# VectorE's share of the exponentials: a chain of ten short steps in place of six, with a new pacing

## The chip, the cores and the metric

The kernel runs on one core of one Trainium2 chip. The metric is the device time of one execution in microseconds (us); with several runs the median is given. TensorE is called PE (PEld is its weight load), VectorE DVE, ScalarE ACT, GpSimd POOL and SyncE SP, as the profile names them.

## The reference

Four transformer attention layers on one sequence of 2048 rows of 640 features, in bf16: layers 0 and 2 look at a sliding window of 256 keys, layers 1 and 3 at all keys. There are 32 heads of 20 features.

```python
def block(x, wqkv, wo, windowed):
    q, k, v = split_heads(x @ wqkv)                 # 32 heads, 20 features each
    scores = einsum("bhqd,bhkd->bhqk", q, k) * 20 ** -0.5
    if windowed:
        scores = where((i - j >= 0) & (i - j < 256), scores, -1e9)
    return merge_heads(softmax(scores) @ v) @ wo

x = x + block(layernorm(x), A_wqkv, A_wo, True)     # layer 0
x = x + block(layernorm(x), B_wqkv, B_wo, False)    # layer 1
x = x + block(layernorm(x), A_wqkv, A_wo, True)     # layer 2
x = x + block(layernorm(x), B_wqkv, B_wo, False)    # layer 3
```

The softmax is computed without subtracting a maximum. Its exponentials are the bulk of the elementwise work: one for each head, query and key.

## The kernel before

**Units and banks.** The sequence is cut into 4 chunks `c` of 512 queries and the heads into 8 groups `g` of 4. A *unit* is the attention of one layer, chunk and group. Its work is a list of *banks*: one bank is the scores of 128 keys by 512 queries for one head, which fills one PSUM bank. A unit of layers 1 and 3 has 16 key blocks by 4 heads, 64 banks; a windowed unit (layers 0 and 2) has 12. Chunk 0 of layers 1 and 3 is computed in parts, whose partial sums are kept in the tile `raw_o`.

**The tiles of the main loop.** The loop (L1269 on) takes three banks at a time, a *tile* (a turn of the loop, called a tick in the code). For each tile, PE computes the scores (L1308) into one of two sets of PSUM banks (0 to 2, or 3 to 6), ACT takes the exponential of the whole tile (L1339) into a tile `pt`, and two or three turns later PE multiplies `pt` with the values (L1373) into PSUM bank 7, which adds up over the unit and is copied out by DVE at its end (L857). In odd turns of the late part a tile can have four banks, if bank 6 is free and no other work wants it. Windowed tiles are multiplied with masks by DVE (L1410).

**The work between.** Layer norm, projections, output projection (L552) and the unit ends run as generators which the loop advances a little in each turn. From about 480 us on, when layer 1 has left its first chunk, all of them share PSUM bank 6: PE writes it, DVE takes the result out (L314, L561, L1048, L1064, L1085), and the next of them may use it. Every engine works through its own instructions in the order in which this program emits them, so a PE instruction that waits for DVE to empty a bank holds back all PE instructions behind it. PE also gets multiplications whose result nobody reads (L634), which keep its clock up.

**Exponentials on DVE.** For most units of layers 1 and 3 with c > 0, the banks of the last key block are taken out of ACT's list: heads 2 and 3 in layer 1 (`aside = (2, 3)`, 24 units, one pair each), all four heads in layer 3 (22 units, two pairs each). They make 68 pairs. The generator `t_side` computes them on DVE, a pair of banks (1024 elements on each of 128 partitions) at a time. The score, scaled by log2(e), becomes an integer whose bits are those of a float: the exponent field gives a power of two, the fraction field goes through a polynomial, and the two are multiplied. The steps of a pair:

- L910, twice: PSUM to integer. In layer 1 the scores were computed as the third bank of a normal tile, which stands in a fixed plan. In layer 3 the generator itself issues the matmul (L903) into bank 6, in odd turns only, and then books bank 6 for two turns.
- L915 and L920: fraction bits and exponent bits.
- L925, L929 and L933: the polynomial, each step `(a op scalar) op b` over two 4-byte tiles.
- L941: the last polynomial step times the power of two, written in bf16 as the pair's output.

PE reads the pair's output at the end of the unit (L1382).

**Pacing.** Each step of `t_side` yields a cost in credit, 0.7 or 1.2. Once in a turn, behind the products with the values, the credit grows by `SIDE_RATE` (late, layer 3) or by 0.4 (before), up to 1.2, and steps are emitted while it is above zero. At a step "bank" the generator stops until a turn in which the scores can be had. `side_done` and `side_need` push the generator on at a unit's end if its pairs are not ready.

**Buffers.** In the middle stage the scratch tiles `xi`, `xm`, `xw` lie in `raw_o` (groups 0 to 5), and groups 6 and 7 are two output pairs. In layer 3 the scratch lies in three of the five `xnT` tiles, which layer norm no longer needs, and three output pairs lie in `ka`.

Of the kernel before, what the change touches and what calls it, by code (L numbers as in the profile page):

```python
# [9 lines left out]
BF16 = mybir.dt.bfloat16  # L10
F32 = mybir.dt.float32
I32 = mybir.dt.int32
ALU = mybir.AluOpType
ACT = mybir.ActivationFunctionType

P = 128
# [5 lines left out]
KD = D // P  # L22
G = 8
C = 512
NC = S // C
EPS = 1e-5
SCALE = DH ** -0.5
# [4 lines left out]

E23 = 2.0 ** 23
LOG2E = 1.4426950408889634
EA, EB, EC, ED = -0.10468731, 1.17604568, 0.83196789, 0.24582313
KA = 18
SIDE_RATE = 0.85
QA = 4

PARTS = {  # L40
# [6 lines left out]
def kernel(  # L47
# [14 lines left out]
    def pool(name, bufs, space=None):  # L62
        kw = {"space": space} if space else {}
        return ctx.enter_context(tc.tile_pool(name=name, bufs=bufs, **kw))
# [5 lines left out]
    xtp = pool("xtp", 5)  # L70
# [34 lines left out]
    op = ps[:, 7, :]  # L105
# [10 lines left out]
    for h in range(2):  # L116
        for n in range(2):
            a = n * D + h * HD
# [10 lines left out]
    def load_wop(w, dense):  # L129
# [9 lines left out]
        out=ident[:], in_=ident[:], compare_op=ALU.not_equal, fill=1.0,  # L139
# [6 lines left out]
    for m, b, ge in (  # L146
# [4 lines left out]
        v = masks[:, m, b * P : (b + 1) * P]  # L151
        nc.gpsimd.affine_select(
            out=v, in_=v, compare_op=ALU.is_ge if ge else ALU.is_gt, fill=0.0,
# [139 lines left out]
    live = Counter()  # L293
# [81 lines left out]
    xnT = {}  # L375
# [491 lines left out]
    side = {"credit": 0.0, "gen": None, "tiles": None, "late": False}  # L867

    def side_start():

        assert live["xnT"] == 0
        tl = [xtp.tile([P, KD, C], BF16, name="xnT", tag="xnT") for _ in range(3)]
        live["xnT"] += 3
        f = [v[:, 0:4, :].rearrange("p a b -> p (a b)") for v in tl[0:3]]
        side["tiles"] = [v.bitcast(F32) for v in f]
        side["out"] = deque(ka_all[:, KA - 6 + 2 * n : KA - 4 + 2 * n, :] for n in range(3))
        side["late"] = True

    def side_early():

        b = part_o["t"]
        side["tiles"] = [b[:, 2 * n : 2 * n + 2, :].rearrange("p a b -> p (a b)") for n in range(3)]
        side["out"] = deque(
            b[:, n, :].bitcast(BF16).rearrange("p (a b) -> p a b", a=2) for n in (6, 7)
        )
        side["gen"] = t_side()
        side_step(False)

    def t_side():

        V = nc.vector
        while aside:
            u = aside[0]
            for pair in range(len(u.aside) // 2):
                while id(u) not in loaded or (u.l == 3 and not side["late"]):
                    yield None
                for i in range(2):
                    yield "bank"
                    xi, xm, xw = side["tiles"]
                    if u.l == 3:  # L900
                        mseq[0] += 1
                        mfree[6] = (state["tick"] + 2, mseq[0])
                        nc.tensor.matmul(  # L903
                            ps[:, 6, :], lhsT=u.k(NT - 1, u.aside[2 * pair + i]),
                            rhs=u.q(u.aside[2 * pair + i], 0, 4), start=True, stop=True,
                        )
                        side["psum"] = ps[:, 6, :]
                    scored = side.setdefault("scored", {})
                    scored[id(u)] = scored.get(id(u), 0) + 1
                    V.tensor_scalar(  # L910
                        out=xi.bitcast(I32)[:, i * C : (i + 1) * C], in0=side["psum"],
                        scalar1=SCALE * LOG2E * E23, scalar2=-128.0 * E23, op0=ALU.mult, op1=ALU.max,
                    )
                    yield 0.7
                V.tensor_scalar(  # L915
                    out=xm.bitcast(I32), in0=xi.bitcast(I32), scalar1=0x7FFFFF, scalar2=0x3E800000,
                    op0=ALU.bitwise_and, op1=ALU.bitwise_or,
                )
                yield 0.7
                V.tensor_scalar(  # L920
                    out=xi.bitcast(I32), in0=xi.bitcast(I32), scalar1=0x7F800000,
                    scalar2=0x40000000, op0=ALU.bitwise_and, op1=ALU.bitwise_xor,
                )
                yield 0.7
                V.scalar_tensor_tensor(  # L925
                    out=xw, in0=xm, scalar=EA, in1=xm, op0=ALU.add, op1=ALU.mult
                )
                yield 1.2
                V.scalar_tensor_tensor(  # L929
                    out=xm, in0=xw, scalar=EB, in1=xm, op0=ALU.mult, op1=ALU.add  # L930
                )
                yield 1.2
                V.scalar_tensor_tensor(  # L933
                    out=xw, in0=xw, scalar=EC, in1=xm, op0=ALU.add, op1=ALU.mult
                )
                yield 1.2
                while not side["out"]:
                    yield None
                pt = side["out"].popleft()
                po = pt.rearrange("p a b -> p (a b)")  # L940
                V.scalar_tensor_tensor(  # L941
                    out=po, in0=xw, scalar=ED, in1=xi, op0=ALU.add, op1=ALU.mult
                )
                side_out.setdefault(id(u), []).append(pt)
                yield 1.2
            aside.popleft()

    def side_step(bank):

        if side["gen"] is None:  # L950
            return False
        moved = False
        while True:
            if side.get("at") == "bank" and not bank:
                return moved
            if side["credit"] <= 0.0:
                return moved
            try:
                at = side["at"] = next(side["gen"])
            except StopIteration:  # L960
                side["gen"] = None
                return moved
            if at is None:
                return moved
            moved = True
            if at == "bank":
                if not bank:
                    return moved
                continue
            side["credit"] -= at  # L970
            if bank:
                return moved
# [223 lines left out]
    with tc.manual_schedule():  # L1196
# [12 lines left out]
        tiles = []  # L1209
        starts = {}  # L1210
        n = 0
# [57 lines left out]
        while ended is None or t < ended + 8:  # L1269
# [3 lines left out]
            if t < len(tiles) or banks:  # L1273
                if t >= len(tiles) and not side["late"] and not live["xnT"] and not todo:
                    side_start()
# [36 lines left out]
                if cur[-1][2] == "side":  # L1312
                    cur = cur[:-1]
                    n_b -= 1
                    if side["gen"] is None:
                        side_early()
                    while side["at"] != "bank":
                        side["credit"] = 0.1
                        assert side_step(False)
                    side["credit"] = max(side["credit"], 0.1)  # L1320
                    side["psum"] = sp[:, n_b, :]
                    side_step(True)
# [11 lines left out]
                while i < n_b:  # L1334
                    b0 = cur[i][3]
                    k = i
                    while k < n_b and cur[k][3] == b0:
                        k += 1
                    nc.scalar.activation(  # L1339
                        out=pt[:, i:k, b0 * P :], in_=sp[:, i:k, b0 * P :],  # L1340
# [50 lines left out]
                    break  # L1391

            if n_b:
                side["credit"] = min(side["credit"] + (SIDE_RATE if side["late"] else 0.4), 1.2)
                side_step(False)

            if t > 0 and masked is not None:
                cur_, pt_ = masked
                i = 0
                while i < len(cur_):  # L1400
# [4 lines left out]
                    if m is not None:  # L1405
# [5 lines left out]
                            out=pt_[:, i:k, cols], in0=pt_[:, i:k, cols], in1=mv_, op=ALU.mult  # L1411
# [38 lines left out]
```

## Time and profile before

| | |
|---|---|
| runs | 2284.01, 2285.57, 2287.35 us |
| median | 2285.57 us |
| the profiled execution | 2284.01 us |
| its span, first to last instruction | 2282.3 us |
| mean granted PE clock | 0.864 |
| exponentials on ACT (L1339) | 1638 instructions, 2096.5 us |
| of these four banks wide | 27 |
| side steps on DVE (L910 to L941) | 544 instructions, 520 us |

The side rows by shape, summed: L910 93.8 us in 136 instructions, L915 and L920 94.4 in 136, L925 to L941 331.5 in 272.

How to read the page: it shows one execution, with the busy time of each engine; then the span cut into 40 equal slices with the busy share of each in tenths, where PEclk is the clock that PE was granted; then groups of equal instructions as "line engine operation written<-read shape xcount | busy us, mean ns of one | idle us of the engine just before them <-who ended it". A list of waits has "engine, what it was about to do <- what it waited for: us in all, times, longest". A table by stage has, for each stretch of time, the busy us and instruction count of PE, PEld, DVE, ACT and POOL, and then the granted clock, the DMA share and GB/s.

### The profile page before, as it was taken

What the parts mean: (1) busy time and instruction counts of PE and PEld (TensorE: products, weight loads), DVE (VectorE), ACT (ScalarE), POOL (GpSimd) and SP (SyncE); (2) the same over time, 40 slices, a digit from 0 to 9 for tenths busy, and PEclk for the clock granted to TensorE, in tenths of its full rate; (3) what the DMA queues carried; (4) which work ended last, traced back from release to release, by engine and by line L of the source; (5) the groups of instructions that cost most, each with busy time, mean ns of one, the idle gap of its engine ahead of it and who ended that gap; (6) DMA issues with size and microseconds to landing.
All of it is one profiled execution on the core that took longest, in us unless ns stands there. A gap on an engine that the chain in (4) does not pass through costs nothing.

```text
span 2282.3 us, 40030 instructions
## 1 busy us (share of the span) xinstructions
PE 1978.4 (87%) x15586; PEld 704.1 (31%) x15746; DVE 1272.2 (56%) x2214; ACT 2169.6 (95%) x1741; POOL 271.0 (12%) x445
## 2 busy tenths in 40 slices
PE   8899999989898998888888998898878888888887
PEld 3343343333233333233332333232221122122222
DVE  6667675435454566455564643432555565666662
ACT  7789899999999999999899999999999999999997
POOL 4323223201100122001210022011000000000000
PEclk9899999999999999999999999999755565556556
DMA  6223223322210233002320043012111111111100
GB/s 193 78 69 101 81 83 90 97 75 56 70 33 14 61 96 93 15 27 64 101 71 14 16 116 95 28 44 74 54 47 30 30 42 30 30 39 41 35 17 15
DMA packets 88284, 135.16 MB, mean 59 GB/s; under 512 B 20766, under 2 KB 63486, under 8 KB 88094
## 3 DMA queue, kind: packets, MB, share of 16 engines
q1 hardware_dynamic: 68878, 79.43, 12.6%
q0 software_dynamic: 19216, 53.17, 7.8%
q8 instruction: 123, 2.02, 0.4%
q14 instruction: 67, 0.55, 0.1%
HBM read 99.52 MB, written 27.79 MB: 56 GB/s over the span
## 4 chain that ended last, share of the span: by engine, by line
ACT 45%; PE 30%; issue 16%; DVE 9%; DMA 0%; ACTq 0%; POOL 0%; SPq 0%; DVEq 0%; POOLq 0%
ACT pt L1339 44%; PE ps L1308 7%; PE ps L364 6%; PE ps L552 5%; PE ps L1373 4%; PE ps L465 3%; DVE pt L1410 2%; PE ps L634 1%; DVE st L314 1%; DVE on L1085 1%; ACT ka L1339 1%; PE ps L1081 1%; DVE x_sb L561 1%; PE ps L429 0%; DVE raw_o L910 0%
## 5 line engine op out<-in xcount | busy, mean ns | idle before, releaser
L1339 ACT ACTIVATE pt<-ps 128x1536 bf16<-128x1536 f32 (+2 forms) x1638 | 2096.5, 1478 | 74.2 <-PE ps L1308 64.9
L1308 PE MATMUL ps<-qt,kt 32*128 32x512 bf16 x4008 | 635.9, 451 | 176.7 <-ACT pt L1339 144.6
L1373 PE MATMUL ps<-pt,vt 128*21 128x512 bf16 x3852 | 462.5, 452 | 7.1 <-issue 4.5
L1308 PEld LDWEIGHTS <-kt 32*128 32x128 bf16 x4008 | 186.0, 93 | 594.1 <-issue 575.7
L1410 DVE TENSOR_TENSOR pt<-pt,masks 128x1024 bf16<-128x1024 bf16 (+6 forms) x403 | 209.5, 554 | 151.0 <-ACT pt L1339 150.5
L634 PE MATMUL ps<-masks,ident 128*128 128x512 bf16 x708 | 243.5, 387 | 27.7 <-DVE on L1085 7.1
L364 PE MATMUL ps<-xnT,wqk 128*128 128x512 bf16 x761 | 206.3, 382 | 19.2 <-DVE on L1085 3.9
L1373 PEld LDWEIGHTS <-vt 128*21 128x21 bf16 x3960 | 99.5, 90 | 337.4 <-issue 325.1
L314 DVE CAST st<-ps 128x512 bf16<-128x512 f32 x134 | 92.7, 692 | 183.8 <-PE ps L364 169.9
L552 PE MATMUL ps<-wop,on 128*128 128x320 bf16 x928 | 165.0, 317 | 8.3 <-DVE x_sb L561 5.2
L910 DVE TENSOR_SCALAR xnT<-ps 128x512 int32<-128x512 f32 x88 | 60.9, 692 | 185.8 <-PE ps L903 185.8
L1308 PE MATMUL ps<-qa,ka 32*128 32x384 bf16 (+2 forms) x1408 | 118.2, 278 | 27.7 <-ACT pt L1339 22.0
L1085 DVE TENSOR_TENSOR on<-on,ps 128x512 bf16<-128x512 bf16 x128 | 86.4, 685 | 65.8 <-PE ps L1081 64.7
L561 DVE TENSOR_TENSOR x_sb<-x_sb,ps 128x320 bf16<-128x320 bf16 x120 | 58.1, 484 | 115.1 <-PE ps L552 114.9
L857 DVE CAST on<-ps 128x512 bf16<-128x512 f32 x112 | 77.1, 688 | 75.1 <-PE ps L1373 48.3
L465 PE MATMUL ps<-wv,xnT 128*128 128x320 bf16 x640 | 110.6, 301 | 7.9 <-DVE on L1085 3.1
L552 PEld LDWEIGHTS <-on 128*128 128x128 bf16 x928 | 84.0, 101 | 77.0 <-issue 47.8
L364 PEld LDWEIGHTS <-wqk 128*128 128x128 bf16 x830 | 69.9, 97 | 111.3 <-issue 53.9
L634 PEld LDWEIGHTS <-ident 128*128 128x128 bf16 x798 | 59.7, 96 | 132.6 <-issue 131.2
L398 POOL TENSOR_SCALAR rstd<-mv 128x4 f32<-128x4 f32 x15 | 4.1, 277 | 776.6 <-DVE mv L385 755.9
L1373 PE MATMUL ps<-pt,va 128*21 128x384 bf16 (+2 forms) x1408 | 75.6, 282 | 3.9 <-DVE pt L1410 1.6
L1308 PEld LDWEIGHTS <-ka 32*128 32x128 bf16 x1408 | 43.0, 92 | 95.9 <-issue 85.9
(101 smaller groups left out, 1585.1 us busy)
## 6 DMA issues: line engine op xcount, KB each, us to landing
vt<-v_d SPq DMA_DIRECT2D x48, 336.0 KB
kt<-k_d SPq DMA_DIRECT2D x192, 80.0 KB
wqk<-in_B_wqkv_dram POOLq DMA_DIRECT2D x80, 160.0 KB, 3.5
wqk<-in_A_wqkv_dram POOLq DMA_DIRECT2D x70, 160.0 KB, 3.4
k_d<-st POOLq DMA_DIRECT2D x75, 128.0 KB, 2.1
q_d<-st POOLq DMA_DIRECT2D x75, 128.0 KB, 2.1
qt<-q_d SPq DMA_DIRECT2D x384, 20.0 KB
v_d<-vs POOLq DMA_DIRECT2D x16, 336.0 KB, 3.0
```

The costliest lines, as they stand in the source:

```text
L314: nc.vector.tensor_copy(out=out_, in_=in_)
L364: nc.tensor.matmul(pq, lhsT=wt[:, dc, :], rhs=xt[:, dc, :], start=(dc == 0), stop=(dc == KD - 1),)
L465: nc.tensor.matmul(pv, lhsT=xt[:, dc, i * P : (i + 1) * P], rhs=wv_sb[l % 2][:, dc, h * HD : (h + 1) * HD], start=(dc == 0), stop=(dc == K ...
L552: nc.tensor.matmul(yp, lhsT=on[:, g, qb * P : (qb + 1) * P], rhs=wop[:, g, i * HD : (i + 1) * HD], start=(g == a), stop=(g == b - 1),)
L561: nc.vector.tensor_tensor(out=xv, in0=had, in1=yp, op=ALU.add)
L634: nc.tensor.matmul(ps[:, b, :], lhsT=ident[:], rhs=masks[:, 0, :], start=True, stop=True)
L857: nc.vector.tensor_copy(out=oT, in_=op)
L1085: nc.vector.tensor_tensor(out=oT, in0=oT, in1=zb, op=ALU.mult)
L1308: nc.tensor.matmul(sp[:, i, col * P : (col + qn) * P], lhsT=u.k(kc, j), rhs=u.q(j, q0, qn), start=True, stop=True,)
L1339: nc.scalar.activation(out=pt[:, i:k, b0 * P :], in_=sp[:, i:k, b0 * P :], func=ACT.Exp, scale=SCALE,)
L1373: nc.tensor.matmul(op[32 * j : 32 * j + VW, q0 * P : (q0 + qn) * P], lhsT=u.v(kc, j), rhs=pg[:, i, col * P : (col + qn) * P], start=(first ...
L1410: nc.vector.tensor_tensor(out=pt_[:, i:k, cols], in0=pt_[:, i:k, cols], in1=mv_, op=ALU.mult)
```

## The change

The chain of a pair is written anew. The integer now carries the float's bias (L910 adds 127 x 2^23 instead of clamping). The fraction is mapped to 1..2 instead of 0.25..0.5. The power of two is cut out by one bit operation and then clamped at zero by a separate step into a new bf16 tile `xe`. The polynomial of fourth degree is evaluated as (y^2 + EB)^2 + EC y + ED with y = EK m + ES, in three one-source steps on 4-byte data, two squares and a sum, and the last step is a product of two bf16 tiles, in place in the output.

Behind the two reads of PSUM a pair had six steps (two with one source, four with two) and has ten (six with one source, three with two 4-byte sources, one with two bf16 sources). The credit of a pair is 9.9 instead of 7.6, and the rates are 1.05 instead of 0.85 (late) and 0.65 instead of 0.4 (before).

The tile `xe` takes the place of one output pair in `raw_o`, so one output pair is left in the middle stage; in layer 3 it lies in a fourth `xnT` tile.

The short name of the change speaks of unit ends normed two at a time, outputs scaled in place and one set of masks; the diff changes nothing in the code of unit ends, scaling or masks.

```diff
-EA, EB, EC, ED = -0.10468731, 1.17604568, 0.83196789, 0.24582313
+EK, ES, EB, EC, ED = (
+    0.34108128280528366, -0.013389613744261132, 0.7155463694844106,
+    0.9531181402314826, 0.010462897723623632,
+)
-SIDE_RATE = 0.85
+SIDE_RATE = 1.05
...
     def side_start():
-        tl = [xtp.tile([P, KD, C], BF16, name="xnT", tag="xnT") for _ in range(3)]
-        live["xnT"] += 3
+        tl = [xtp.tile([P, KD, C], BF16, name="xnT", tag="xnT") for _ in range(4)]
+        live["xnT"] += 4
         f = [v[:, 0:4, :].rearrange("p a b -> p (a b)") for v in tl[0:3]]
-        side["tiles"] = [v.bitcast(F32) for v in f]
+        side["tiles"] = [v.bitcast(F32) for v in f] + [tl[3][:, 0:2, :].rearrange("p a b -> p (a b)")]
...
     def side_early():
-        side["out"] = deque(
-            b[:, n, :].bitcast(BF16).rearrange("p (a b) -> p a b", a=2) for n in (6, 7)
-        )
+        side["tiles"].append(b[:, 6, :].bitcast(BF16))
+        side["out"] = deque([b[:, 7, :].bitcast(BF16).rearrange("p (a b) -> p a b", a=2)])
...
     def t_side():
                     V.tensor_scalar(
                         out=xi.bitcast(I32)[:, i * C : (i + 1) * C], in0=side["psum"],
-                        scalar1=SCALE * LOG2E * E23, scalar2=-128.0 * E23, op0=ALU.mult, op1=ALU.max,
+                        scalar1=SCALE * LOG2E * E23, scalar2=127.0 * E23, op0=ALU.mult, op1=ALU.add,
                     )
                     yield 0.7
                 V.tensor_scalar(
-                    out=xm.bitcast(I32), in0=xi.bitcast(I32), scalar1=0x7FFFFF, scalar2=0x3E800000,
+                    out=xm.bitcast(I32), in0=xi.bitcast(I32), scalar1=0x7FFFFF, scalar2=0x3F800000,
                     op0=ALU.bitwise_and, op1=ALU.bitwise_or,
                 )
                 yield 0.7
                 V.tensor_scalar(
-                    out=xi.bitcast(I32), in0=xi.bitcast(I32), scalar1=0x7F800000,
-                    scalar2=0x40000000, op0=ALU.bitwise_and, op1=ALU.bitwise_xor,
+                    out=xi.bitcast(I32), in0=xi.bitcast(I32), scalar1=-0x800000, scalar2=None,
+                    op0=ALU.bitwise_and,
                 )
                 yield 0.7
-                V.scalar_tensor_tensor(out=xw, in0=xm, scalar=EA, in1=xm, op0=ALU.add, op1=ALU.mult)
-                yield 1.2
-                V.scalar_tensor_tensor(out=xm, in0=xw, scalar=EB, in1=xm, op0=ALU.mult, op1=ALU.add)
-                yield 1.2
-                V.scalar_tensor_tensor(out=xw, in0=xw, scalar=EC, in1=xm, op0=ALU.add, op1=ALU.mult)
-                yield 1.2
+                V.tensor_scalar(out=xe, in0=xi, scalar1=0.0, scalar2=None, op0=ALU.max)
+                yield 0.7
+                V.tensor_scalar(out=xm, in0=xm, scalar1=EK, scalar2=ES, op0=ALU.mult, op1=ALU.add)
+                yield 0.7
+                V.tensor_tensor(out=xw, in0=xm, in1=xm, op=ALU.mult)
+                yield 1.2
+                V.tensor_scalar(out=xw, in0=xw, scalar1=EB, scalar2=None, op0=ALU.add)
+                yield 0.7
+                V.tensor_tensor(out=xw, in0=xw, in1=xw, op=ALU.mult)
+                yield 1.2
+                V.tensor_scalar(out=xm, in0=xm, scalar1=EC, scalar2=ED, op0=ALU.mult, op1=ALU.add)
+                yield 0.7
...
-                V.scalar_tensor_tensor(out=po, in0=xw, scalar=ED, in1=xi, op0=ALU.add, op1=ALU.mult)
+                V.tensor_tensor(out=po, in0=xw, in1=xm, op=ALU.add)
+                yield 1.2
+                V.tensor_tensor(out=po, in0=po, in1=xe, op=ALU.mult)
                 side_out.setdefault(id(u), []).append(pt)
-                yield 1.2
+                yield 0.7
...
-                side["credit"] = min(side["credit"] + (SIDE_RATE if side["late"] else 0.4), 1.2)
+                side["credit"] = min(side["credit"] + (SIDE_RATE if side["late"] else 0.65), 1.2)
                 side_step(False)
```

## The prediction

> **What bounds the kernel now.** I first read the busy table, then the slices, then busy time by stage.
>
> ```profile
> PE 1978.4 (87%) x15586; PEld 704.1 (31%) x15746; DVE 1272.2 (56%) x2214; ACT 2169.6 (95%) x1741; POOL 271.0 (12%) x445
> DVE  6667675435454566455564643432555565666662
> ACT  7789899999999999999899999999999999999997
> PEclk9899999999999999999999999999755565556556
> ```
>
> ScalarE (ACT) is busy 95% of the span, nearly all of it the exponentials of L1339. The change touches only VectorE (DVE), at 56%. So the question is not what DVE costs, but how often DVE makes TensorE (PE) late enough to leave ACT without scores. The busy time by stage (columns: us, then busy us of PE, PEld, DVE, ACT, POOL) separates the two places where DVE makes exponentials:
>
> ```profile
> 480.00:1320.00 840.00, 742.47 (x6146) 278.82 (x6224) 464.22 (x817) 818.29 (x641) 90.88 (x142) 1.00 0.20 55
> 1690.00:2230.00 540.00, 446.07 (x2795) 113.95 (x2791) 333.13 (x407) 534.84 (x391) 0.00 (x0) 0.53 0.11 33
> ```
>
> The first is the middle stage (layers 1 and 2 woven, 24 DVE pairs), the second the late stage (layer 3, 44 pairs). ACT is idle for 21.7 us of the first and 5.2 of the second; DVE is busy 55% and 62%. What the side work costs stands in the groups of DVE by shape:
>
> ```profile
> L941 DVE SCALAR_TENSOR_TENSOR ka<-xnT 128x1024 bf16<-128x1024 f32 x44 | 53.8, 1223 | 1.1
> L929 DVE SCALAR_TENSOR_TENSOR xnT<-xnT 128x1024 f32<-128x1024 f32 x44 | 53.7, 1221 | 0.9
> L910 DVE TENSOR_SCALAR xnT<-ps 128x512 int32<-128x512 f32 x88 | 60.9, 692 | 185.8 <-PE ps L903 185.8
> L915 DVE TENSOR_SCALAR xnT<-xnT 128x1024 int32<-128x1024 int32 x44 | 30.5, 693 | 1.4
> L1410 DVE TENSOR_TENSOR pt<-pt,masks 128x1024 bf16<-128x1024 bf16 x98 | 66.6, 684 | 36.8 <-ACT pt L1339 36.6
> ```
>
> The reader sees two prices for 1024 elements: about 0.69 us for one SBUF source, 1.22 for two 4-byte sources. And L910 shows slack: in the late stage DVE stands 185.8 us (4.2 per pair) waiting for the matmul of L903.
>
> **The change part by part.** *Constants, names.* The four numbers of the polynomial become five; no cost. *The two reads of PSUM (L910)* keep form and size: 2 x 0.692 us before and after.
>
> *The chain behind them.* Before: two bit operations (0.694 each) and four two-source operations (1.22): 2 x 0.694 + 4 x 1.22 = 6.27 us a pair. After: six one-source operations (and/or, and, max, three multiply or add), three two-source ones on 4-byte data (two squares, one sum) and one product of 2-byte data: 6 x 0.694 + 3 x 1.22 + 0.684 = 8.51. The change adds 2.24 us of DVE to a pair: 24 x 2.24 = 54 us in the middle stage, 44 x 2.24 = 99 in the late one, 152 in all; DVE busy goes to about 1424 us.
>
> *What of this the trace doesn't show.* The four arithmetic one-source operations (max with 2-byte output among them) are not in it. Upper end 1.22, the two-source row; lower end 0.684, the mask row. I take 0.694, from the bit operations of the same instruction, size and source width. The three two-source ones could be as cheap as the mask row (0.684) and no dearer than 1.22, which I take: L929 reads the same tiles. So the addition lies between 2.24 - 3 x 0.54 = +0.6 and 2.24 + 4 x 0.53 = +4.3 us a pair.
>
> *The pacing.* The generator asks 0.7 or 1.2 of credit a step: 7.6 for a pair before, 9.9 after, while a late tile now earns 1.05 instead of 0.85. I walked both by hand from a second PSUM read with the credit at its cap of 1.2. Before: the last step goes out five tiles on, and the next pair's first read, which needs an odd tile, comes at the eighth. After: the last goes out seven tiles on with 0.05 of credit left, so the next read still comes at the eighth. Ten tiles a pair either way; the trace agrees, with reads of L910 starting at 1742.9, 1756.8 and 1770.3 us and tiles of 1.40 us (12.56 for nine). In the middle stage (0.4 against 0.65) the last step goes out eleven tiles behind the second read in both. So I expect PE, ACT and every DMA queue to get the same instructions in the same order; only DVE's stream grows, by 4 x 68 = 272.
>
> *Buffers.* A fourth xnT tile is taken when none is in use; one is left over. In the middle stage raw_o keeps one output pair instead of two. The output is written some twelve tiles into a unit, when the unit before has long been read, so no wait is added; if that cover were gone, DVE would stand at the sum with every evacuation of PSUM bank 6 behind it, up to the 10 us between 524.3 and 535.4 in which the first pair now lies ready.
>
> *What leaks to the end.* Side steps go to DVE behind the tile's PV products, just ahead of the next tile's evacuation of bank 6, which PE needs back. In the middle stage this looks so (start, us, idle before):
>
> ```profile
> 1119.06 0.69 DVE L314 CAST st<-ps 128x512 bf16<-128x512 f32 x1 [1.33 <-PE ps L364]
> 1119.66 1.22 DVE L933 SCALAR_TENSOR_TENSOR raw_o<-raw_o 128x1024 f32<-128x1024 f32 x1
> 1121.08 0.69 DVE L314 CAST st<-ps 128x512 bf16<-128x512 f32 x1 [0.20 <-PE ps L364]
> ```
>
> Between evacuations DVE idles 1.33 us; a long step fits with 0.20 left, a short one with more, and two steps or a step beside a unit's end do not. Say that the added work is late where DVE is busy anyway: 54 x 0.55 = 30 us in the middle, 99 x 0.62 = 61 late. PE is mostly ahead. These are ACT's waits in the middle stage:
>
> ```profile
> ACT pt L1339 <- PE ps L1308: 19.2, 53, 0.9
> ```
>
> 53 of 641 exponentials waited, 8%; in the late stage about 15 of 450, 3.3% (1605 us on). Leaks: 30 x 0.08 = 2.5 us and 61 x 0.033 = 2.0. Queues grow faster than load: DVE's idle share falls from 0.45 to 0.38 (x 1.17) and from 0.38 to 0.20 (x 1.9), so I take 2.9 and 3.8, together +6.7. With +0.6 a pair it is 1.5; with +4.3, by the same ratio, 13. On the profiled execution's 2284.0 us (span 2282.3 and 1.7 around it) the centre gives 2290.7; the median of the runs lies 1.6 higher, so I forecast between the two readings, 2291.
>
> *A rule against the change.* The Trainium skill, "VectorE: DVE Perf Modes", section "Rules for kernel authors", says of chained DVE work: "Minimize op *count*, not sems". The rows side with it only in part: a short step costs 0.694 where a long one costs 1.22. By its fixed part of some 150 cycles (0.156 us at its 0.96 GHz) four more operations would be 42 us of the DVE time, an estimate from that page. The page "SBUF — State Buffer", section "SBUF: two separate sides", warns that a DVE operation which uses two ports keeps GpSimd from writing DMA descriptors; in the middle stage POOL issues 112 DMAs, and 24 x 4 x 0.694 = 67 us more of such operations in 840 would hold them some 112 x 0.08 x 0.35 = 3 us in all, an estimate by that page which no row here shows.
>
> **The rivals.** *All of it is hidden.* For it: 4.2 us of DVE slack per late pair against 2.24 added, and PE's matmuls wait 0.7 us for DVE from 1605 us to the end. Against it: the middle stage, where PE waits in many small pieces for L1085, L314 and L561. It gives no change, 2283 to 2290.
>
> *Faster: short steps make better room.* Between evacuations of L465 DVE idles 0.93 to 0.94 us: a step of 0.694 fits there, one of 1.22 overruns by 0.28. A middle pair has four long steps before, three after: 24 x 0.28 = 6.7 us at most, 2279. Against it: five more steps of 0.69 come along, and the late stage has no such rows.
>
> *Slower: DVE becomes the bound of layer 3.* A late pair comes every (2217.4 - 1610.4 - 2.7) / 43 = 14.1 us. DVE is busy 0.617 x 14.1 = 8.7 us of it, 10.9 after at my prices. It decides from 14.1 - 8.7 = 5.4 us of addition on, or earlier, if the side's reads come so late that bank 6 is not free for PE. At the upper price (+4.3) DVE has 1.1 us left in a pair; if unit ends and the waits for L903 then cost each pair 0.3 to 0.8 us, 44 pairs lose 13 to 35 us: 2299 to 2321, centre 2308.
>
> *The words are not what is done.* They name norming, scaling in place and masks; the diff touches none of L1048, L1085 or L1410. Those rows should stay, and the time then comes from the other cases alone, so it has no chance of its own.
>
> **How the numbers follow.** About 0.2% (4.6 us) is what a measurement of this kernel can tell from no change. The forecast, a small leak, gets 0.55: its own range is 2286 to 2299, and some two thirds of it lies above 2290.1 (0.37 slower, 0.18 same). All hidden: 0.20 (0.17 same, 0.02 slower, 0.01 faster). Faster: 0.11 (0.10 faster, 0.01 same). DVE the bound: 0.14, slower. Together faster 0.11, same 0.36, slower 0.53. The range, 2281 to 2304, leaves out about half of the faster case and two thirds of the DVE-bound one.
>
> **What would show it.** Right: DVE busy near 1424 us with one-source steps at 0.69, two-source ones at 1.22 and the last product at 0.68; L1339 unchanged in count; pairs still every 14 us late; idle before L1339 up by 5 to 8 us, mostly for L1308; DVE's wait at L903 down by about 80 us. Wrong: a one-source step near 1.2, pairs twelve tiles apart (the 0.05 of credit missed), 2048-wide exponentials other than 27, PE waiting at L903 or L1382, or a time below 2284.

## The result, and the profile after

| | before | after |
|---|---|---|
| median of the runs | 2284.79 us (4 runs) | 2296.28 us (4 runs) |
| lowest to highest | 2283.59 to 2287.35 | 2293.98 to 2301.73 |
| profiled execution, its span | 2284.01, 2282.3 | 2301.73, 2300.0 |

The changed kernel is slower: ratio 1.0052, interval 1.0032 to 1.0072, or 11.5 us between the medians. The profiled execution of after is the slowest of its four, so its span holds some 5 us that the median does not. On the page of after, the busy table that answers to that of before:

```profile
PE 1990.8 (87%) x15586; PEld 706.1 (31%) x15746; DVE 1411.6 (61%) x2486; ACT 2172.0 (94%) x1741; POOL 273.7 (12%) x445
```

ACT's work is the same (2172.0 against 2169.6 us, 1741 instructions each), DVE has 272 instructions and 139 us more. PE, ACT, POOL and SP have the same instructions in the same order as before; only DVE's stream differs. So nearly all that was lost, 15.3 of the 17.7 us between the two spans, is time in which ACT stood idle. The groups of the new steps in DVE's table by shape of after:

```profile
L927 DVE TENSOR_SCALAR xnT<-xnT 128x1024 bf16<-128x1024 f32 x44 | 30.5, 694 | 1.4
L935 DVE TENSOR_SCALAR xnT<-xnT 128x1024 f32<-128x1024 f32 x44 | 30.4, 691 | 1.0
L933 DVE TENSOR_TENSOR xnT<-xnT 128x1024 f32<-128x1024 f32 x44 | 53.8, 1222 | 0.9
L950 DVE TENSOR_TENSOR ka<-ka,xnT 128x1024 bf16<-128x1024 bf16 x44 | 30.4, 690 | 1.3
L912 DVE TENSOR_SCALAR xnT<-ps 128x512 int32<-128x512 f32 x88 | 60.8, 691 | 112.3 <-PE ps L905 111.8
```

Every price is as it was taken from before: one source 0.69 us (with a 2-byte output too), two 4-byte sources 1.22, the 2-byte product 0.69. The last row is the late stage's slack: DVE still waits 111.8 us for the side matmul, 74 less than before. Late pairs still come every (2233.4 - 1624.4 - 2.7) / 43 = 14.1 us.

Where the time went is seen by matching the n-th exponential of both traces (start in before, how much later it starts in after, both in us from the span's start):

```
before     517.4   586.5   788.7   822.4  1059.5  1093.7  1618.7  2038.7  2267.8
after later  1.7     5.6     6.1    10.9    11.6    14.2    13.9    14.2    17.4
```

The lag grows in jumps, not evenly. The first 1.7 us lie ahead of the first side step. Then it grows by 3.9 us between 517 and 587, 4.8 between 789 and 822, and 2.7 between 1060 and 1094. Between the jumps hardly anything is lost; the last 3 us are lost late, behind 2039 us, around the output projection there and in the last units. Busy time by stage shows what the largest jump is. First before, where the stretch from 805 holds the same layer norm, then after (columns as above, the clock is the fourth number from the end):

```profile
805.00:835.00 30.00, 27.62 (x229) 11.79 (x228) 19.68 (x38) 28.16 (x21) 6.22 (x12) 1.00 0.32 89
```

```profile
812.00:817.00 5.00, 3.11 (x25) 1.22 (x24) 4.00 (x10) 5.00 (x5) 2.27 (x6) 0.97 0.66 144
817.00:822.00 5.00, 4.87 (x29) 1.90 (x29) 3.44 (x8) 2.65 (x3) 0.81 (x1) 0.50 0.21 70
822.00:827.00 5.00, 4.96 (x31) 1.95 (x28) 2.18 (x6) 3.94 (x3) 0.00 (x0) 0.51 0.01 3
```

From 812 to 817 us PE is busy 3.11 us of 5; then it is granted half its clock, is busy nearly all the time and does fewer matmuls (29 and 31 in 5 us, where before has 229 in 30, or 38 in 5), and ACT, which needs its scores, is busy 2.65 and 3.94 of 5 us. The trace of after has four such stretches of half clock in the middle stage, at 547.0, 584.6 and 1100.0 us (3.4 us each) and at 816.7 (10.2 us); the trace of before has none between 129 and 1610 us. (Two more in after, at 230 and 342 us, lie ahead of the first side step at 506 us, so the change did not make them; the run without a polynomial below has them too.)

What goes before the half clock, in order of time (start, us, engine and line, idle before and who ended it; here and in the next such lists, rows of undisturbed work in between are left out):

```profile
813.18 0.68 DVE L935 TENSOR_SCALAR raw_o<-raw_o 128x1024 f32<-128x1024 f32 x1
813.28 1.47 POOL L404 TENSOR_TENSOR rstd<-rstd,nhalf 128x4 f32<-128x4 f32 x1
...
814.78 0.16 DVE L407 SCALAR_TENSOR_TENSOR nmr<-mv,rstd 128x4 f32<-128x4 f32 x1 [0.93 <-POOL rstd L404]
814.98 0.56 DVE L414 TENSOR_SCALAR xn<-x_sb,rstd,nmr 128x640 bf16<-128x640 bf16 x1
...
815.47 1.21 DVE L937 TENSOR_TENSOR raw_o<-raw_o 128x1024 f32<-128x1024 f32 x1
816.60 0.48 DVE L317 CAST vs<-ps 128x320 bf16<-128x320 f32 x1
817.00 0.43 DVE L414 TENSOR_SCALAR xn<-x_sb,rstd,nmr 128x640 bf16<-128x640 bf16 x1
817.13 0.59 PE L637 MATMUL ps<-masks,ident 128*128 128x512 bf16 x1 [1.58 <-DVE vs L317]
...
819.43 1.45 ACT L1346 ACTIVATE pt<-ps 128x1536 bf16<-128x1536 f32 x1 [1.65 <-PE ps L1315]
```

A side step (L935) starts 0.1 us ahead of the layer norm's power on POOL (L404), which takes 1.47 us. DVE has come to `nmr`, which needs that result, and stands 0.93 us with everything behind it in its queue: the normed row, a square of the side chain (1.21 us), and only then the evacuation of PSUM bank 6 (L317). PE stands 1.58 us in front of that bank, its clock is halved, and ACT waits 1.65 us and more. Before, at the same layer norm:

```profile
806.07 1.03 POOL L401 TENSOR_TENSOR rstd<-rstd,nhalf 128x4 f32<-128x4 f32 x1
806.36 0.49 DVE L314 CAST vs<-ps 128x320 bf16<-128x320 f32 x1 [0.66 <-PE ps L465]
806.77 1.22 DVE L929 SCALAR_TENSOR_TENSOR raw_o<-raw_o 128x1024 f32<-128x1024 f32 x1
...
807.90 0.16 DVE L404 SCALAR_TENSOR_TENSOR nmr<-mv,rstd 128x4 f32<-128x4 f32 x1
```

There the power takes 1.03 us, ends while DVE is at an evacuation and a side step, and `nmr` has nothing to wait for.

### The profile page after: what moved, and what is told of

The parts are those of the page before. It is cut to its first block, busy times and chain, and to the rows that moved or that the text cites. A ratio compares the mean times of both kernels' runs of the same rounds, so it can differ in the third digit from the quotient of the medians.

```text
span 2300.0 us, 40298 instructions
## 1 busy us (share of the span) xinstructions
PE 1990.8 (87%) x15586; PEld 706.1 (31%) x15746; DVE 1411.6 (61%) x2486; ACT 2172.0 (94%) x1741; POOL 273.7 (12%) x445
## 3 DMA queue, kind: packets, MB, share of 16 engines
q8 instruction: 123, 2.02, 0.4%
## 4 chain that ended last, share of the span: by engine, by line
ACT 42%; PE 29%; issue 16%; DVE 11%; POOL 1%; DMA 0%; ACTq 0%; SPq 0%; DVEq 0%; POOLq 0%
ACT pt L1346 41%; PE ps L1315 7%; PE ps L367 5%; PE ps L555 5%; PE ps L1380 4%; PE ps L468 3%; PE ps L637 2%; DVE pt L1417 2%; DVE on L1092 1%; DVE st L317 1%; ACT ka L1346 1%; PE ps L1088 1%; DVE x_sb L564 1%; PE ps L432 1%; DVE on L860 0%
## 5 line engine op out<-in xcount | busy, mean ns | idle before, releaser
L1346 ACT ACTIVATE pt<-ps 128x1536 bf16<-128x1536 f32 (+2 forms) x1638 | 2098.3, 1468 | 88.9 <-PE ps L1315 80.5
L637 PE MATMUL ps<-masks,ident 128*128 128x512 bf16 x708 | 245.3, 389 | 33.6 <-DVE on L1092 8.4
L317 DVE CAST st<-ps 128x512 bf16<-128x512 f32 x134 | 92.7, 692 | 178.9 <-PE ps L367 168.9
L912 DVE TENSOR_SCALAR xnT<-ps 128x512 int32<-128x512 f32 x88 | 60.8, 691 | 112.3 <-PE ps L905 111.8
L367 PEld LDWEIGHTS <-wqk 128*128 128x128 bf16 x830 | 70.0, 97 | 111.8 <-issue 54.2
L637 PEld LDWEIGHTS <-ident 128*128 128x128 bf16 x798 | 60.2, 97 | 136.0 <-issue 134.4
```

What stands on the lines that cost most here:

```text
L317: nc.vector.tensor_copy(out=out_, in_=in_)
L367: nc.tensor.matmul(pq, lhsT=wt[:, dc, :], rhs=xt[:, dc, :], start=(dc == 0), stop=(dc == KD - 1),)
L637: nc.tensor.matmul(ps[:, b, :], lhsT=ident[:], rhs=masks[:, 0, :], start=True, stop=True)
L1346: nc.scalar.activation(out=pt[:, i:k, b0 * P :], in_=sp[:, i:k, b0 * P :], func=ACT.Exp, scale=SCALE,)
```

## The experiments

All were timed in the same way as before and after, each beside runs of the kernel before on its chip; "before" below is their median. The ratio and its interval are taken from all runs, so a loss worked out from the ratio can differ by 1 or 2 us from the difference of the medians.

| run | median us | before | ratio | interval | half-clock stretches, 480 to 1330 us |
|---|---|---|---|---|---|
| middle_only | 2295.3 | 2286.5 | 1.0043 | 1.0030 to 1.0056 | 4 |
| late_only | 2286.2 | 2286.5 | 1.0008 | 0.9996 to 1.0020 | 0 |
| idle3 | 2296.4 | 2286.5 | 1.0045 | 1.0033 to 1.0057 | 3 |
| no_poly | 2283.3 | 2286.5 | 0.9985 | 0.9976 to 0.9993 | 0 |
| after_hold | 2292.8 | 2285.9 | 1.0031 | 1.0018 to 1.0044 | 2 |
| after_rate09 | 2324.5 | 2285.9 | 1.0179 | 1.0161 to 1.0196 | 8 |
| after_warm195 | 2297.1 | 2285.9 | 1.0054 | 1.0042 to 1.0067 | 3 |
| late_more | 2284.9 | 2285.9 | 0.9997 | 0.9987 to 1.0007 | 0 |
| after_rate05 | 2289.5 | 2285.9 | 1.0021 | 1.0008 to 1.0034 | 1 |
| before_rate065 | 2299.9 | 2285.9 | 1.0059 | 1.0047 to 1.0071 | 3 |
| before_rate09 | 2306.6 | 2285.9 | 1.0085 | 1.0063 to 1.0107 | 3 |
| after_rate05_hold | 2289.7 | 2285.9 | 1.0015 | 1.0006 to 1.0023 | 2 |

The last column is from the one profiled execution of each. In all runs but late_more and after_warm195 every engine but DVE keeps before's order.

### In which stage

The chain was changed in one stage at a time.

```diff
+                if u.l == 1:        # middle_only; late_only: u.l == 3
+                    ...             # ten steps
+                else:
+                    ...             # six steps
```

> The ten-step chain, its buffers and the rate 0.65 in the middle stage only (layer 1), the old chain and 0.85 in layer 3. PE, ACT, POOL and SP keep the order of before. Theory A (clock: DVE's added work holds back PE at bank 6 in a few places of the middle stage, PE's activity falls, its clock is halved for 3.4 us or more, and each such stretch costs ACT 1.5 to 5 us): 5 to 9 us slower than before, in a few jumps that coincide with half-clock stretches. Theory B (plain queueing, as predicted: many small waits of PE for DVE, spread out, the clock stays full): about 3 us slower, in small pieces. Theory C (the half-clock stretches are chance and have nothing to do with the change): as before, within 2 us.

> The ten-step chain and the rate 1.05 in layer 3 only, the old chain, two output pairs and 0.4 in the middle stage. Theory A: 2 to 4 us slower, lost where layer 3 does its output projections and at the end, where PE runs behind; the rest of the late stage, in which ACT is never idle, loses nothing. Theory B: about 4 us slower, spread over the stage. Theory C: as before, within 2 us. If the middle and the late part add up, the two differences together give the whole change (about 11 us).

The middle stage alone loses 0.43%, 9.8 us (8.8 between the medians): most of the change. Its four half-clock stretches lie where after's lie (545.3, 582.9, 815.0 for 10.2 us, 1098.3), in another execution. The late stage alone can't be told from before (0.08%, interval -0.04 to +0.20%), although it carries 99 of the 152 us of new DVE work. In its late stage:

```profile
1690.00:2230.00 540.00, 445.07 (x2784) 112.90 (x2784) 413.09 (x563) 534.22 (x390) 0.00 (x0) 0.53 0.12 33
```

DVE is busy 413 of 540 us instead of 333, and ACT 534.2 instead of 534.8. The runs show neither the 2 to 4 us that theory A expected at the output projections nor the 4 us of theory B, spread queueing; but the interval reaches 4.6 us, so neither is excluded.

### Is it DVE time, or the new chain

```diff
+                for _ in range(3):
+                    V.tensor_scalar(out=xm, in0=xm, scalar1=1.0, scalar2=None, op0=ALU.mult)
+                    yield 0.7
                 V.scalar_tensor_tensor(
-SIDE_RATE = 0.85
+SIDE_RATE = 1.05
-... (SIDE_RATE if side["late"] else 0.4)
+... (SIDE_RATE if side["late"] else 0.65)
```

> The old chain with three more one-source steps a pair, which multiply the fraction by 1 (0.69 us each, so 8.35 us behind the reads instead of 6.27; the change has 8.51), with the rates of the change (0.65 and 1.05) and the old buffers. If the loss is DVE time in the queue (theories A and B), it loses what the change loses, 8 to 12 us. If it comes from something in the new chain itself (the fourth tile, the single output pair, the forms of its operations), it is as before, within 2 us.

```diff
                 V.tensor_scalar(... bitwise_xor ...)
                 yield 0.7
-                V.scalar_tensor_tensor(out=xw, in0=xm, scalar=EA, in1=xm, ...)
                 yield 1.2
-                V.scalar_tensor_tensor(out=xm, in0=xw, scalar=EB, in1=xm, ...)
                 yield 1.2
-                V.scalar_tensor_tensor(out=xw, in0=xw, scalar=EC, in1=xm, ...)
                 yield 1.2
```

> The kernel before with the three middle polynomial steps left out (the last step takes the fraction itself, so the exponentials of the side pairs are wrong); the credit still counts them, so every other engine keeps its order. DVE has 3.66 us less a pair, 249 us in all. Theory A and B: the waits that DVE causes in before shrink, 1 to 4 us faster than before. Theory C: the same as before. If the loss by the change were linear in DVE time (11 us for 152), this would be 18 us faster; I expect far less, because before shows little waiting for DVE.

The old chain with three multiplications by one and the rates of the change, on the old buffers, loses 0.45%: it is not the form of the chain, the fourth tile or the single output pair. Steps and rates were changed together here; before_rate065 below, which changes the middle stage's rate alone, tells them apart. Taking 249 us of DVE work away gains 0.15% (3 us), far less than in proportion: in before hardly anything hangs on the time of the side steps any more.

### What sets the loss off

The side steps were paused around a layer norm's `rstd`.

```diff
         nc.gpsimd.tensor_tensor(out=rstd[:], in0=rstd[:], in1=nhalf[:], op=ALU.pow)
+        side["hold"] = True
         yield ("wait", 2)
...
         rows = deque([normed(0)])
         yield ("wait", 1)
+        side["hold"] = False
...
-                side_step(False)
+                if not side.get("hold"):
+                    side_step(False)
```

> The changed kernel, but the side steps pause from the moment a layer norm gives its rstd to POOL until its first rows are normed (some three turns, once a chunk). PE, ACT, POOL and SP keep their order; of DVE's stream 20 instructions move. Theory A' (what is lost in the middle stage are collisions of a side step with the layer norm: rstd on POOL is late, DVE stands at nmr, the evacuation of bank 6 behind it is late, PE stands, its clock halves): rstd takes 1.04 us in all places, the half-clock stretches at 547, 817 and 1100 us are gone, the one at 585 (no layer norm there) stays; 2286 to 2290 us. Theory B' (the amount of DVE work counts, wherever it falls): still 2294 to 2297.

Partly so. The power on POOL takes 1.03 to 1.04 us in all places of the middle stage, the long stretch at 817 and the one at 1100 are gone, the one without a layer norm stays (587.0). But the loss only falls from 11.5 us to 6.8 (0.52% to 0.31%, with intervals that overlap), and one stretch that I expected to vanish has only moved (547 to 553). Its trace says why:

```profile
548.89 0.84 DVE L931 TENSOR_SCALAR raw_o<-raw_o 128x1024 f32<-128x1024 f32 x1
...
549.76 1.22 DVE L935 TENSOR_TENSOR raw_o<-raw_o 128x1024 f32<-128x1024 f32 x1
...
550.90 0.44 DVE L415 TENSOR_SCALAR xn<-x_sb,rstd,nmr 128x640 bf16<-128x640 bf16 x1
551.26 0.48 DVE L317 COPY xnT<-ps 128x640 bf16<-128x640 bf16 x1
...
551.79 0.38 PE L639 MATMUL ps<-masks,ident 128*128 128x512 bf16 x1 [1.46 <-DVE xnT L317]
```

Two side steps and a normed row now stand ahead of the next evacuation of bank 6, and PE stands 1.46 us. The collision with `rstd` is one way for DVE to be late at bank 6, not the only one.

More fillers were tried against the falling clock.

```diff
-                warmth = 1.76 if state["unit"] >= woven else 1.0
+                warmth = 1.95 if state["unit"] >= woven else 1.0
```

> The changed kernel with more matmuls that nobody reads (warmth 1.95 instead of 1.76, 95 matmuls more). If the clock falls for want of PE work in general, it stays full and the time is 2287 to 2291. If it falls because PE stands in front of bank 6 (theory A'), fillers don't help: they go to bank 6 too and wait there; the stretches at 547, 817 and 1100 stay, and the time is that of the changed kernel or 1 to 3 us more.

They don't help (2297.1). Half-clock stretches follow at 544, 582 and 1094 us. The fillers go to bank 6 themselves: L637 is mostly the instruction that stands.

The long stretch is missing in this execution, against the expectation, and that tells the wait from the clock. The same collision stands there (the power takes 1.47 us, `nmr` waits 0.93), with the same wait of PE:

```profile
815.05 0.38 PE L637 MATMUL ps<-masks,ident 128*128 128x512 bf16 x1 [1.59 <-DVE vs L317]
...
816.47 4.13 ACT L1346 ACTIVATE pt<-ps 128x1536 bf16<-128x1536 f32 x3 [0.76 <-PE ps L1315]
```

But the clock stays full:

```profile
815.00:820.00 5.00, 4.00 (x41) 2.12 (x40) 4.08 (x8) 4.24 (x4) 0.81 (x1) 1.00 0.23 74
820.00:825.00 5.00, 4.82 (x43) 2.01 (x41) 2.55 (x5) 4.66 (x4) 0.00 (x0) 1.00 0.00 0
```

ACT is busy 4.24 and 4.66 of 5 us behind the wait, where after has 2.65 and 3.94. Between the exponentials that start at 789 and 822 us in before, the lag grows by 1.7 us here and by 4.8 in after: the wait costs ACT about 1.7 us, the half clock of 10.2 us about 3 more (one execution of each; after_warm195 has more fillers besides). A wait of 1.02 us at a unit's end (582 us) makes a second pair: the lag grows by 1.7 us around it in after, where half clock of 3.4 us follows, and by 0.3 in before_rate065 below, where none does. Around the four waits of after it grows by 1.8, 1.7, 4.8 and 2.6 us, 10.9 of the 12.2 between 517 and 1619 us.

### The amount or the pace

First the changed kernel with more credit per turn in the middle stage.

```diff
-... (SIDE_RATE if side["late"] else 0.65)
+... (SIDE_RATE if side["late"] else 0.9)       # after_rate09; after_rate05: 0.5
```

> The changed kernel with 0.9 instead of 0.65 of credit in the middle stage: the same DVE work, done in fewer turns, so other steps fall on the layer norms. Theory A': the half-clock stretches move, appear or vanish, and the time goes with them, anywhere between 2286 and 2300. Theory B': as after, 2294 to 2297, or more, because the steps are denser; the stretches at 547, 585, 817 and 1100 stay.

I had expected shifted collisions; the loss more than trebled, to 38.5 us, with the same DVE work. The lag grows in jumps and also in between. These are rows of PE's waits in the middle stage; in before the same waits (there L634 for DVE at L1085, L1048 and L314) come to 3.5 us for the first of the three and 0.4 us for each of the others:

```profile
PE ps L637 <- DVE on L1092: 12.1, 21, 1.7
PE ps L637 <- DVE rz L1055: 6.0, 8, 1.1
PE ps L637 <- DVE vs L317: 5.6, 6, 1.6
```

So the pace was put to the test from both sides: the changed kernel slower, and the kernel before, without any added work, faster.

```diff
-... (SIDE_RATE if side["late"] else 0.4)
+... (SIDE_RATE if side["late"] else 0.65)      # before_rate065; before_rate09: 0.9
```

> The changed kernel with 0.5 instead of 0.65 of credit in the middle stage: the same ten steps, spread over some 15 turns behind the second read instead of 12. Theory P (what counts is how much DVE work is put into one turn, so the pace of 0.65 costs and not the 54 us as such): the loss falls by half or more, 2287 to 2292. Theory W (the amount counts, wherever it falls): as the change, 2295 to 2297. Theory A' alone (only which step falls on a layer norm): anything between 2286 and 2300, with the half-clock stretches in other places.

> The kernel before, its six steps, with only the middle stage's rate at 0.65 instead of 0.4: no DVE work is added, it is done in 7 turns instead of 12. Theory P: slower than before by about what the change loses, 2292 to 2298, with half-clock stretches in the middle stage. Theory W: as before, 2284 to 2287. Theory A' alone: anything.

> The kernel before with the middle stage's rate at 0.9. The changed kernel at 0.9 lost 39 us. Theory P: 15 to 40 us slower than before. Theory W: as before, 2284 to 2288.

Theory W is refuted. What theory P forecast came in two of the three runs, and in the third, before_rate065, the loss is even 2 us above its range. The kernel before at 0.65 loses 0.59%, 14.0 us between the medians, as much as the change, with not one DVE instruction added; the changed kernel at 0.5 loses 0.21% (eleven runs from 2286.4 to 2297.0 us). A', which allowed any time, is not refuted by these times: a faster pace also moves the steps to other places. But after_hold, whose power on POOL is never late, still loses 0.31%, so the layer norm is not all of it. In the trace of before_rate065 the collision looks as in after, with the old chain's steps:

```profile
812.89 1.21 DVE L933 SCALAR_TENSOR_TENSOR raw_o<-raw_o 128x1024 f32<-128x1024 f32 x1
812.99 2.00 POOL L401 TENSOR_TENSOR rstd<-rstd,nhalf 128x4 f32<-128x4 f32 x1
...
815.02 0.16 DVE L404 SCALAR_TENSOR_TENSOR nmr<-mv,rstd 128x4 f32<-128x4 f32 x1 [0.93 <-POOL rstd L401]
...
815.71 1.21 DVE L941 SCALAR_TENSOR_TENSOR raw_o<-raw_o 128x1024 bf16<-128x1024 f32 x1
816.84 0.48 DVE L314 CAST vs<-ps 128x320 bf16<-128x320 f32 x1
...
817.37 0.59 PE L634 MATMUL ps<-masks,ident 128*128 128x512 bf16 x1 [2.12 <-DVE vs L314]
```

Here a two-source step lies beside the power, which takes 2.00 us, and PE stands 2.12. At 0.65 the amount doesn't show beside the pace: 14.0 us are lost with the six steps, 9.9 with the nine of idle3, 11.5 with the ten. At 0.9 it does: 20.7 us with the six steps, 38.5 with the ten.

> The changed kernel with both repairs: 0.5 in the middle stage and no side steps while a layer norm waits for its rstd. If the loss is pace and collisions, both repairs together bring it near before: 2286 to 2289. If it is the amount, 2292 or more.

Both repairs together leave 0.15%, not clearly better than the slower pace alone (0.21%). What is left may be the amount; the intervals don't settle it, and the ten steps at before's rate of 0.4 were not run.

### Using DVE's room in layer 3

Since the late stage has DVE to spare, eight more pairs were given to it, with before's chain.

```diff
+                    self.more = (0, 1) if l == 3 and g % 3 == 0 else ()
...
+            self.sides = [(NT - 2, j) for j in self.more] + [(NT - 1, j) for j in self.aside]
```

> The kernel before (old chain) with 8 more pairs on DVE in layer 3 (heads 0 and 1 of the key block before the last, in the groups 0, 3 and 6), taken out of ACT's list, at a rate of 1.05; a fourth xnT tile gives two more output pairs. If layer 3 is bound by ACT alone and has room on DVE, as the run with the new chain in layer 3 only says, 16 banks of 0.465 us leave ACT: 7 us faster than before, 2278 to 2280. If DVE or bank 6 is the next limit, no gain or a loss.

No gain (0.9997). ACT has 5.7 us less work on the page (2163.9 instead of 2169.6), but from 1605 us on it waits longer for PE, before (two rows of its list of waits) and then late_more:

```profile
ACT pt L1339 <- PE ps L1308: 10.4, 15, 1.6
ACT pt L1339 <- PE ps L903: 1.7, 1, 1.7
```

```profile
ACT pt L1344 <- PE ps L1313: 15.0, 24, 2.0
```

That is 3 of the 6 us. Where the rest went was not followed. No run of this study that computes all of the reference is shown to be faster than the kernel before.

## Why the prediction was right, and where not

**Direction and range: right, in part by luck; the size: about half.** 2291 was forecast in 2281 to 2304, and 2296.3 was measured: 11.5 us more than before, where the sum of leaks gave 6.7. The range was made wide for the unknown prices of the new steps, and these came as taken. What was wrong was the cost of the middle stage, which happened to fit into that width, and it came about in another way than forecast. The idle time before the exponentials, given as a sign, grew by 14.7 us in the profiled execution (74.2 to 88.9) and not by 5 to 8, though mostly for the scores, as forecast.

**Prices: right.** One-source steps 0.69, two-source 1.22, product 0.69; DVE 1412 us busy against some 1424; the wait at L903 74 us shorter against about 80.

**Order and period: right.** Four engines keep their order, late pairs come every 14.1 us, and there are still 27 four-bank exponentials (besides the 1638 of the table of before, not among them). The step that hung on 0.05 of credit was not missed.

**The leak of the middle stage: too small.** "Leaks: 30 x 0.08 = 2.5 us", raised to 2.9, became 9.8 us (middle_only; 8.8 between the medians). The term treated PE's waits as many small ones, of which ACT feels 8%. They are few and long. In before's middle stage PE never stands longer than 0.9 us at a time; in after it does four times (1.86, 1.02, 1.58 and 1.83 us), and each time its clock is halved for 3.4 us or more beside it. The wait of 1.58 us with its half clock costs 4.8, where the same wait at full clock costs 1.7 (after_warm195). The clock was on the page, at 9 in every slice from 114 us to 1598, and the forecast did not ask what would take it away.

**The leak of the late stage: not settled.** 3.8 us were forecast. late_only shows 0.08%, 1.8 us, with an interval from -0.9 to 4.6 us that holds both zero and the forecast; behind 1619 us the profiled executions lose 3.5 us (after) and 1.4 us (late_only). The share of the added work is small in any case, at most 4.6 of 99 us. A likely reason, which no run tests: the clock is at half there anyway (0.53), PE is mostly ahead of ACT, and DVE's queue empties while it waits for the side matmul.

**The pacing: wrong.** It was taken as harmless because the last step goes out at the same turn and the others keep their order. But that the ten steps end on time is bought by more DVE work in each turn, and this is what costs: the rate alone, with no step added, loses 14.0 us, as much as the whole change (before_rate065).

**The rule on two ports.** It was weighed for DMA descriptors, at 3 us. What showed was the same sharing at another place: in the middle stage the power on POOL takes 1.03 to 1.05 us when no side step has just started, 1.47 or 1.49 with a one-source step started 0.1 us earlier, and 2.00 to 2.02 with a two-source one. It agrees with what the Trainium skill, "SBUF — State Buffer", section "SBUF: two separate sides", says of the port that the two engines share, with a DVE operation of two SBUF inputs as well. The other direction, which the section has too, is not seen here: in before a side step (L929) starts 0.7 us into the power and takes its usual 1.22 us. The 3 us for DMA descriptors were tested by no run.

**The rivals.** DVE as the bound of layer 3 did not come: 111.8 us of waiting are left there. "Short steps make better room" was not seen. That all is hidden may hold for the late stage (0.08%, the interval holds zero); in the middle one 0.21% are left even at half a credit a turn.

## What to carry to other kernels

In this kernel, the work that one engine does on the side was not priced by its sum, nor by the share of the time in which the engine is idle, but first of all by how much of it is put between two instructions that another engine waits for; when a side chain gets longer, let it end later before you make it denser. Where PE works densely at full clock, look for the single wait of one or two microseconds: in after, four such waits (1.0 to 1.9 us), each with half clock beside it, made the exponentials 1.7 to 4.8 us later apiece. Fillers that need the same buffer as the work they fill for stand in the same queue.

## What the runs showed of the hardware

A single wait of PE of 1.0 to 2.8 us in a row of otherwise dense work can be met by half clock: of the 33 half-clock stretches in the profiled middle stages of this study (14 traces), 31 lie beside a wait of PE of 0.6 us or more, mostly over 1; the two others (841 us in after_rate05_hold, 1005 us in before_rate09, the longest of all) follow several waits of 0.3 to 0.5. Nor is a long wait sure to do it: the same wait of 1.02 us at a unit's end (582 us in after) was met by half clock in five of the kernels and not in before_rate065, and the wait of 1.58 us of after (817 us) stands as 1.59 at 815 us in after_warm195, where the clock stays full. The lengths are 3.4 us, or 6.8, 10.2 and 23.9. The Trainium skill, "TensorE: Matmul & The Clock Gate", "Part 1: The HAM clock gate (the "warmup" mystery)", speaks of a window of 3413 ns that runs freely; the lengths agree with it, and a free window would explain why one and the same wait does not always halve the clock, but no run here shows the window itself.

A two-source or one-source DVE step on 4-byte data that starts 0.1 us ahead of the 128x4 power on POOL delays its end to about 0.9 us past the step's own end (from 813.18 + 0.68 to 814.75 in after, from 812.89 + 1.21 to 814.99 in before_rate065), so a 16-byte row per partition on one engine can hang on a 4 KB one on another.
